# Another order of the opening in a fused retention and two-layer kernel on one core

## The chip, the core and the metric

The kernel runs on one NeuronCore of a Trainium2 chip. The metric is the time of one execution on the device, in microseconds (us). A kernel is run several times, and the median counts; one more execution is recorded by the hardware profiler, and all views of the trace come from that one. Five engines work side by side, each on its own queue and strictly in the order of that queue: TensorE (PE: matrix products), VectorE (DVE), ScalarE (ACT), GpSimd (POOL) and SyncE (SP), which here only issues DMA transfers.

## What is computed

Retention over 4 x 8 heads of 768 tokens and 64 dimensions, and behind it two dense layers with a leaky rectifier between them:

```python
gamma = 1.0 - 2.0 ** (-5.0 - np.arange(H))
scale = 1.0 / np.sqrt(D)
for t in range(S):
    state = gamma[None, :, None, None] * state + np.einsum('bhd,bhe->bhde', k[:, :, t], v[:, :, t])
    y[:, :, t] = scale * np.einsum('bhd,bhde->bhe', q[:, :, t], state)
x = y.transpose(0, 2, 1, 3).reshape(B * S, H * D)      # 3072 x 512
h = x @ w_in                                           # 512 x 2048
g = np.maximum(h, 0.0) + alpha * np.minimum(h, 0.0)
out = g @ w_out                                        # 2048 x 512
```

All inputs and the output are float32 in HBM; products are taken in float16 and summed in float32.

## The kernel before

**Units.** The retention is cut into 24 units `w` (0 to 23). A unit holds 256 tokens of one sequence and four of its eight heads; a pair of units makes 256 tokens, and four units make a block of 512 tokens. There are six blocks. A sequence of 768 tokens is three pairs of units, and a state is handed from pair to pair (and between the two chunks of 128 tokens in a unit).

**What is done for a unit.** `load` fetches k, q and v (256 KB each) through SyncE's queue. `prep` scales k and q into a float16 tile `kdq` (line 189). For units 0 to 7, `turn` brings it into the other layout by eight transposes on TensorE into a PSUM bank `trb` (line 232) and a copy by ScalarE (`kq`, line 238); for later units a DMA transposes. `cast_v` or the last line of `prep` casts v to `vx`. `scores` are 16 small products (line 260) into the PSUM pair `sc`; `masked` multiplies them with a mask on VectorE (line 295). `state_sums` are small products of k and v (line 284), from which `state` makes the carried state on VectorE (lines 309, 311). `within` multiplies masked scores by v into the PSUM pair `y` (line 344) and adds the carried states of one half (line 322); a tiny instruction of another engine, the teller, says that these are through (lines 357, 359); `finish` adds the other half and lets ScalarE copy the result as `xT`, the input of the dense layers (line 373). `visit(w_old, w_new)` runs `within` of an old unit, `scores` and `state_sums` of a new one, `finish` of the old one, then `masked` and `state` of the new one.

**The dense layers of a block.** `ffn1` makes 16 slices `ft` of 128 hidden features; a slice is four products of 128 x 512 (line 427), a rectified copy by ScalarE (line 407) and a combination by VectorE (line 396) into `gt`. `ffn2` makes the four tiles of 128 tokens of the output; a tile is 16 products of 128 x 512 (line 444), one for each slice of `w_out`, summed in one PSUM bank, which ScalarE empties (line 453). Both are generators: `tick(gen, m)` issues the next m products, and so the order of TensorE's instructions is written out by hand, with the units' work between the ticks. In blocks 1 to 5 the next block's units stand between the products of `ffn2`, with fixed numbers of ticks.

**Weights.** `fetch` brings w_in and w_out in 16 pieces of 256 KB each through the same queue of SyncE and in the same staging buffers as k, q and v (eight buffers for each of the three); `cast_w` casts a piece to float16 on GpSimd (line 179). The order of loads in SyncE's queue, and of casts in GpSimd's queue, is that of the program.

**PSUM.** There are eight banks: two single banks named fa and fb, two in a pool "p", and two pairs "s" and "y". The letters in the string given to `ffn1` say which bank each of the 16 slices takes (a capital is the second half of the pair).

**The opening**, lines 467 to 584, is written out unit by unit: units 0 to 3 with turns on TensorE, fills (`busy`, products of ones that nobody reads, line 217) between them, `ffn1(0)` with its first steps between units 2 and 3, then `ffn2(0)` with units 4 to 7 between its products. In `ffn2(0)` tiles 0 and 1 go side by side (one product of each in turn for a slice), then tile 2, then tile 3. The loads stand in the order: w_in, k and q of unit 4, w_out's first four pieces, v of unit 4, the other twelve pieces of w_out, units 5 to 11.

Of the kernel before, what the change touches and what calls it, by code (L numbers as in the profile page):

```python
# [9 lines left out]
FP = mybir.dt.float32  # L10
F16 = mybir.dt.float16
# [7 lines left out]
def kernel(  # L19
# [15 lines left out]
    nc = tc.nc  # L35
# [7 lines left out]
    WB = 4  # L43
# [34 lines left out]
    sbp = ctx.enter_context(tc.tile_pool(name="sbp", bufs=1, space=bass.MemoryType.SB))  # L78
# [6 lines left out]
    ident = mi[:, 256:384]  # L85
    alpha_sb = sbp.tile([NFT, 128], FP, tag="alpha", name="alpha")
    warm = sbp.tile([128, 128], FP, tag="warm", name="warm")[:, 0:1]
    ones = sbp.tile([128, 256], F16, tag="ones", name="ones")[:, 0:128]
    word = sbp.tile([128, 128], FP, tag="word", name="word")[:, 0:1]
    bell = sbp.tile([128, 128], FP, tag="bell", name="bell")[:, 0:1]  # L90
    oma_sb = sbp.tile([128, 128], FP, tag="oma", name="oma")[:, 0:NFT]
# [2 lines left out]

    NPE = 8

    flip = [0]

    def ps(name, tag, n=512, dt=FP, bufs=2):
        if tag == "f":  # L100
            tag = ("fa", "fb")[flip[0] % 2]
            flip[0] += 1
        if tag in ("fa", "fb"):
            bufs = 1
        return psp.tile([128, n], dt, tag=tag, bufs=bufs, name=name)

# [70 lines left out]
    def cast_w(which, i, j):  # L177
        dst, t = pieces[which, i, j]
        nc.gpsimd.tensor_copy(out=dst, in_=t)  # L179
# [33 lines left out]

    def busy(m, at):

        for _ in range(m):
            nc.tensor.matmul(out=at[:, 0:128], lhsT=ones, rhs=ones, start=True, stop=True)

    def cast_v(w):
        vx, v_in = v_ins.pop(w)  # L220
        nc.scalar.activation(out=vx, in_=v_in, func=COPY, bias=0.0, scale=1.0)

    def turn(w, tag, kinds=(0, 1), fill=0):

        kdq, kq, vx = prepped[w]
        flat = kdq.rearrange("p k z r d -> p (k z r d)")
        bank = ps("trb", tag)
        busy(fill, bank)
        trb = bank.bitcast(F16)
        lo, hi = 4 * kinds[0], 4 * kinds[-1] + 4  # L230
        for i in range(lo, hi):
            nc.tensor.transpose(  # L232
                out=trb[:, 128 * i : 128 * i + 128],
                in_=flat[:, 128 * i : 128 * i + 128],
                identity=ident,
            )
        cols = slice(128 * lo, 128 * hi)
        nc.scalar.activation(  # L238
            out=kq.rearrange("p b i -> p (b i)")[:, cols],
            in_=trb[:, cols],  # L240
            func=COPY,
            bias=0.0,
            scale=1.0,
        )
# [25 lines left out]
    sums = {}  # L270
# [2 lines left out]
    def chunks(w):  # L273
        return (0,) if place(w)[3] == NUS - 1 else (0, 1)

    def state_sums(w, cs=None):
        kdq, vx = raw[w]
        for c in cs or chunks(w):
            sums[w, c] = ps(f"st{c}", "p")
        for x in range(2):  # L280
            for a in range(2):
                for c, r in DIAG:
                    if c in (cs or chunks(w)):
                        nc.tensor.matmul(  # L284
                            out=sums[w, c][half(r), 64 * x : 64 * x + 64],
                            lhsT=kdq[half(c), 0, 2 * x + a, r, :],
                            rhs=vx[half(c), 2 * r + x, a, :],
                            start=(a == 0),
                            stop=(a == 1),
                        )  # L290

    def masked(w):
        kdq, kq, vx, sc = live[w]
        m2 = sbp.tile([128, 4, 2, 128], F16, tag="m2", bufs=2, name="m2")
        nc.vector.tensor_tensor(  # L295
            out=m2.rearrange("p s a i -> p s (a i)"),
            in0=sc.rearrange("p (s n) -> p s n", n=256),
            in1=mask.unsqueeze(1).to_broadcast([128, 4, 256]),
            op=MULT,
        )  # L300
        live[w][3] = m2

    def state(w, cs=None):
        u, g, b, c3 = place(w)
        decay = tab[:, 32 + 2 * g : 34 + 2 * g].unsqueeze(2).to_broadcast([128, 2, D])
        for c in cs or chunks(w):
            stv = sums.pop((w, c))[:, 0:128].rearrange("p (x e) -> p x e", e=D)
            if c3 + c > 0:
                nc.vector.tensor_tensor(out=stv, in0=tgs[2 * u + c, g], in1=stv, op=ADD)  # L309
            tg = sbp.tile([128, 4, D], F16, tag="tg", bufs=8, name="tg")[:, 0:2, :]  # L310
            nc.vector.tensor_tensor(out=tg, in0=stv, in1=decay, op=MULT)  # L311
            tgs[2 * u + c + 1, g] = tg
# [20 lines left out]
                    after = None  # L333
        return ins

    def within(w, mid=None, teller=None):
        u, g, b, c3 = place(w)
        vx, m2 = live[w][2:4]
        y = ps("y", "y", 1024, FP, 1)
        started = set()  # L340
        for r in range(2):
            for a in range(2):
                for c, x in DIAG:
                    nc.tensor.matmul(  # L344
                        out=y[half(x), 256 + 256 * c + 128 * r : 384 + 256 * c + 128 * r],
                        lhsT=vx[half(c), 2 * r + x, a, :],
                        rhs=m2[half(c), 2 * r + x, a, :],
                        start=(c, x) not in started,
                        stop=(a == 1 and c3 + c == 0),
                        skip_group_check=True,  # L350
                    )
                    started.add((c, x))
        if mid:
            mid()
        last = carried(w, y, started, True)
        if teller != nc.scalar:
            done = (teller or nc.vector).memset((warm if teller is None else bell)[0:1], 0.0)  # L357
        else:
            done = teller.activation(
                out=word[0:1], in_=word[0:1], func=COPY, bias=0.0, scale=1.0  # L360
            )
        behind(done, last, "tells that the products within the chunks are through")
        live[w].append((y, started, done))

    def finish(w):
        u, g, b, c3 = place(w)
        y, started, done = live[w].pop()
        carried(w, y, started, False, done)
        live.pop(w)
        n, i = divmod(u, 2)  # L370
        if w % WB == 0:
            xT[n] = sbp.tile([128, 2, 4, 2, 128], F16, tag="xT", bufs=2, name=f"xT{n}")
        nc.scalar.activation(  # L373
            out=xT[n][:, g, 2 * i : 2 * i + 2].rearrange("p c r (i a) -> p (c r) i a", a=2),
            in_=y[:, 256:768].rearrange("p (s a i) -> p s i a", a=2, i=64),
            func=COPY,
            bias=0.0,
            scale=1.0,
        )

    def visit(w_old, w_new, cs=None):
        if w_old is not None:
            within(w_old)
        if w_new is not None:
            scores(w_new)
            state_sums(w_new, cs)
        if w_old is not None:
            finish(w_old)
        if w_new is not None:
            masked(w_new)  # L390
            state(w_new, cs)

    gts = {}
# [66 lines left out]
    def tick(gen, m):  # L460
        for _ in range(m):
            if next(gen, 1) == 1:
                return
# [37 lines left out]
    cast_v(1)  # L501
    within(0, teller=nc.scalar)
    turn(2, "f", (0,), fill=4)
    finish(0)
    turn(2, "f", (1,), fill=3)
    state_sums(1)
    prep(3, opening=True, k_on=nc.gpsimd)
    state(1)
    scores(2, fill=8)
    masked(2)  # L510
    within(1, teller=nc.gpsimd)
    for j in range(4):
        cast_w("wi", 0, j)
    cast_v(2)
    turn(3, "f", (0,))
    turn(3, "f", (1,), fill=2)
    finish(1)
    cast_v(3)
# [1 line left out]
    state(2, (0,))  # L520
    scores(3, fill=5)
    masked(3)
    gen = ffn1(0, "ffspypSffYppsfyS", (2, 4))
    within(2, teller=nc.scalar)
    tick(gen, 4)
    finish(2)
    state_sums(3, (0,))
    state(3, (0,))
    tick(gen, 4)
    within(3, mid=lambda: tick(gen, 2))  # L530
    tick(gen, 2)
    finish(3)
    for j in range(4):
        fetch("wi", 3, j)
    load(4, "kq")
    for i in range(4):
        for j in range(4):
            fetch("wo", i, j)
        if i == 0:
            load(4, "v")  # L540
    for w in range(WB + 1, 3 * WB):
        load(w)
    for i in range(1, 4):
        for j in range(4):
# [1 line left out]
    prep(4, opening=True, k_on=nc.gpsimd)  # L546
    for i in range(4):
        for j in range(4):
            cast_w("wo", i, j)

    for _ in gen:
        pass
    turn(4, "p")
    cast_v(4)
    gen = ffn2(0, ((0, 1), (2,), (3,)), ("fa", "fb", "fa", "fb"))
    state_sums(2, (1,))
    state(2, (1,))
    tick(gen, 5)
    state_sums(3, (1,))
    state(3, (1,))  # L560
    visit(None, 4)
    prep(5, opening=True, q_on=nc.vector)
    tick(gen, 27)
    turn(5, "p")
    cast_v(5)
    prep(6, opening=True)
    tick(gen, 5)
    visit(4, 5)
    tick(gen, 3)
    turn(6, "p")  # L570
    cast_v(6)
    prep(7, opening=True)
    tick(gen, 6)
    turn(7, "fb")
    cast_v(7)
    visit(5, 6)
    tick(gen, 9)
    visit(6, 7)
    tick(gen, 5)
    within(7)  # L580
    tick(gen, 2)
    finish(7)
    for _ in gen:
        pass
# [10 lines left out]
    for n in range(1, NBLK):  # L595
        gen = ffn1(n)
# [5 lines left out]
        gen = ffn2(n)  # L602
# [48 lines left out]
```

## Time and profile before

| | before |
|---|---|
| median of 3 runs | 214.1 us (213.47 to 215.0) |
| profiled execution: time | 213.6 us |
| profiled execution: span of its instructions | 211.8 us |
| TensorE busy | 205.5 us (97%) |
| VectorE, ScalarE, GpSimd busy | 125.4, 99.2, 70.9 us |
| HBM read, written | 27.45 MB, 6.29 MB |

The span runs from the first to the last instruction of the program; 1.8 us of the execution's time lie around it. Starts in the views are counted from the beginning of the span. In a row of the order of time stand the start, the length, the engine, the line, the operation, what it writes and reads, shapes, and the count of merged instructions; in brackets the idle time before it and what ended it. TensorE's products are pipelined, so their lengths overlap, and a product of 128 x 512 shows some 0.38 us though the next one starts 0.216 us behind it. So gaps are read from starts, and a busy share of 97% does not say that 97% of the span is needed.

### The profile page before, as it was taken

The page shows a single profiled execution, that of the slowest core. Times are in us where ns is not written, and L with a number is a line of the kernel's source. Part 1 is how long each engine was busy: PE and PEld are TensorE (multiplying, and loading weights), DVE is VectorE, ACT ScalarE, POOL GpSimd, SP SyncE. Part 2 cuts the span into 40 slices and gives each one's busy share as a digit, 9 for nine tenths or more (in the row PEclk, how much of TensorE's full clock was granted, in tenths as well). Part 3 has the DMA queues.
Part 4 walks back from the last instruction along what each step waited for, and adds up shares of the span by engine and source line. Part 5 has one row for each costly group of instructions (what it writes and reads, how often), then busy time and mean ns, then how long its engine had stood idle before and what let it go on. Part 6 is the DMA issues. An engine that isn't in the chain of part 4 may idle for free.

```text
span 211.8 us, 5285 instructions
## 1 busy us (share of the span) xinstructions
PE 205.5 (97%) x2175; PEld 103.8 (49%) x2175; DVE 125.4 (59%) x224; ACT 99.2 (47%) x168; POOL 70.9 (33%) x94
## 2 busy tenths in 40 slices
PE   7999999899999999999999999999999999999992
PEld 8775454364444554444554444554444554444440
DVE  2773986356588733588644588534588733588000
ACT  2685762464765223665223665223665223665121
POOL 0569798349927563544040265000000000000000
PEclk9999999999999999999999999999999999999998
DMA  6999999999999995991364993324500111100111
GB/s 193 348 375 386 304 396 396 300 296 315 321 221 315 274 227 157 263 294 35 88 212 104 218 270 107 89 63 104 147 6 0 50 53 53 50 0 0 53 77 71
DMA packets 63832, 38.28 MB, mean 181 GB/s; under 512 B 19120, under 2 KB 57152, under 8 KB 63808
## 3 DMA queue, kind: packets, MB, share of 16 engines
q1 hardware_dynamic: 63488, 37.76, 62.5%
q8 instruction: 17, 0.28, 0.6%
q10 hardware_dynamic: 320, 0.19, 0.3%
q14 instruction: 7, 0.06, 0.1%
HBM read 27.45 MB, written 6.29 MB: 159 GB/s over the span
## 4 chain that ended last, share of the span: by engine, by line
PE 76%; DMA 13%; POOL 4%; SPq 4%; issue 1%; ACT 0%
PE ops L444 36%; PE hps L427 33%; DMA wo<-in_moe_w_out_dram 6%; SPq L149 4%; PE y L344 3%; DMA wi<-in_moe_w_in_dram 3%; DMA vs<-in_v_dram 3%; PE sc L260 2%; DMA qs<-in_q_dram 2%; POOL win L179 2%; POOL wout L179 1%; PE y L322 1%; PE st L284 1%; POOL kdq L189 1%; ACT os L453 0%
## 5 line engine op out<-in xcount | busy, mean ns | idle before, releaser
L444 PE MATMUL ops<-wout,gt 128*128 128x512 f16 x384 | 89.6, 380 | 0.0
L396 DVE SCALAR_TENSOR_TENSOR gt<-hm,oma,hps 128x512 f16<-128x512 f32 x96 | 71.2, 747 | 28.2 <-ACT hm L407 18.6
L427 PE MATMUL hps<-xT,win 128*128 128x512 f16 (+1 forms) x392 | 84.7, 375 | 0.0
L407 ACT ACTIVATE hm<-hps 128x512 f32<-128x512 f32 x96 | 57.0, 597 | 24.8 <-PE hps L427 24.4
L427 PEld LDWEIGHTS <-win 128*128 128x128 f16 x392 | 37.9, 98 | 44.7 <-issue 0.3
L444 PEld LDWEIGHTS <-gt 128*128 128x128 f16 x384 | 34.9, 98 | 39.8 <-issue 0.5
L189 POOL TENSOR_TENSOR kdq<-ks,tab 128x512 f16<-128x512 f32 x19 | 19.8, 1043 | 42.2 <-DMA ks<-in_k_dram 38.1
L373 ACT ACTIVATE xT<-y 128x512 f16<-128x512 f32 x24 | 14.3, 597 | 40.4 <-PE y L322 40.0
L295 DVE TENSOR_TENSOR m<-sc,mi 128x1024 f16<-128x1024 f32 x24 | 29.3, 1222 | 3.2 <-PE sc L260 1.0
L453 ACT ACTIVATE os<-ops 128x512 f32<-128x512 f32 x24 | 14.2, 597 | 36.1 <-PE ops L444 36.1
L189 POOL TENSOR_TENSOR kdq<-qs,tab 128x512 f16<-128x512 f32 x22 | 23.3, 1058 | 12.0 <-DMA qs<-in_q_dram 12.0
L357 DVE MEMSET warm<- 1x1 f32 x21 | 1.2, 59 | 25.7 <-PE y L322 25.7
L311 DVE TENSOR_TENSOR tg<-st,tab 128x128 f16<-128x128 f32 x40 | 11.6, 289 | 2.0 <-PE st L284 0.9
L322 PE MATMUL y<-kq,tg 64*64 64x128 f16 x160 | 11.5, 228 | 0.0
L179 POOL CAST win<-wi 128x512 f16<-128x512 f32 x16 | 9.8, 613 | 3.3 <-DMA wi<-in_moe_w_in_dram 2.9
L309 DVE TENSOR_TENSOR st<-tg,st 128x128 f32<-128x128 f16 x32 | 9.3, 291 | 2.5 <-PE st L284 0.6
L344 PEld LDWEIGHTS <-vx 64*64 64x64 f16 x384 | 6.4, 106 | 8.6 <-issue 6.6
L260 PE MATMUL sc<-kq 64*64 64x128 f16 x384 | 10.0, 218 | 0.5 <-ACT kq L238 0.3
L238 ACT ACTIVATE kq<-trb 128x512 f16<-128x512 f16 (+1 forms) x12 | 8.6, 735 | 3.5 <-PE trb L232 3.4
L344 PE MATMUL y<-m,vx 64*64 64x128 f16 x384 | 10.0, 221 | 0.1
L179 POOL CAST wout<-wo 128x512 f16<-128x512 f32 x16 | 9.6, 613 | 1.4 <-DMA wo<-in_moe_w_out_dram 1.1
L209 POOL CAST vx<-vs 128x512 f16<-128x512 f32 x16 | 9.8, 610 | 0.5 <-PE ops L444 0.2
(26 smaller groups left out, 66.1 us busy)
## 6 DMA issues: line engine op xcount, KB each, us to landing
ks<-in_k_dram SPq DMA_DIRECT2D x24, 256.0 KB, 4.2
qs<-in_q_dram SPq DMA_DIRECT2D x24, 256.0 KB, 4.6
vs<-in_v_dram SPq DMA_DIRECT2D x24, 256.0 KB, 4.6
out_dram<-os SPq DMA_DIRECT2D x24, 256.0 KB, 2.5
wi<-in_moe_w_in_dram SPq DMA_DIRECT2D x16, 256.0 KB, 5.4
wo<-in_moe_w_out_dram SPq DMA_DIRECT2D x16, 256.0 KB, 5.7
kq<-kdq SPq DMA_TRANSPOSE x16, 4.2
mi<-mi_const ACTq DMA_DIRECT2D x1, 128.0 KB, 2.9
```

The costliest lines, as they stand in the source:

```text
L179: nc.gpsimd.tensor_copy(out=dst, in_=t)
L189: eng.tensor_tensor(out=kdq[:, kind].rearrange("p z r d -> p r z d"), in0=src.rearrange("p (r x) (a d) -> p r (x a) d", a=2, x=2), in1=tab ...
L260: nc.tensor.matmul(out=sc[half(c), at : at + 128], lhsT=kq[half(r), 2 * x + a, half(c)], rhs=kq[half(r), 4 + 2 * x : 6 + 2 * x, half(c)], ...
L295: nc.vector.tensor_tensor(out=m2.rearrange("p s a i -> p s (a i)"), in0=sc.rearrange("p (s n) -> p s n", n=256), in1=mask.unsqueeze(1).to_ ...
L322: ins = nc.tensor.matmul(out=y[half(x), 256 + 256 * c + 128 * r : 384 + 256 * c + 128 * r], lhsT=tgs[2 * u + c, g][half(r), x, :], rhs=kq[ ...
L344: nc.tensor.matmul(out=y[half(x), 256 + 256 * c + 128 * r : 384 + 256 * c + 128 * r], lhsT=vx[half(c), 2 * r + x, a, :], rhs=m2[half(c), 2 ...
L373: nc.scalar.activation(out=xT[n][:, g, 2 * i : 2 * i + 2].rearrange("p c r (i a) -> p (c r) i a", a=2), in_=y[:, 256:768].rearrange("p (s ...
L396: nc.vector.scalar_tensor_tensor(out=gt[:, ft, lo:hi], in0=hm, scalar=oma_sb[:, ft : ft + 1], in1=hps, op0=MULT, op1=ADD,)
L407: nc.scalar.activation(out=hm, in_=hps, func=RELU, bias=0.0, scale=-1.0)
L427: nc.tensor.matmul(out=hpss[ft][:, 128 * lo : 128 * hi], lhsT=w_in_all[:, hp, 128 * ft : 128 * ft + 128], rhs=xT[n][:, hp // 2, lo:hi, hp ...
L444: nc.tensor.matmul(out=opss[tq], lhsT=gt[:, ft, 128 * tq : 128 * tq + 128], rhs=w_out_all[:, ft, :], start=(ft == 0), stop=(ft == NFT - 1),)
L453: nc.scalar.activation(out=os_sb, in_=opss[tq], func=COPY, bias=0.0, scale=1.0)
```

## The change

It has these parts:

- **Fills:** four fills of 128 columns become one of 512 (`ones` is 512 wide), and some counts change.
- **PSUM names:** "p" becomes two single banks pa and pb in turn, which may also be named one by one; `state_sums` takes a bank or a slice of one, and `within` may use the pair "s".
- **Opening of units 0 to 3:** unit 2's second turn goes ahead of `finish(0)`, unit 3's first turn ahead of `scores(2)`; unit 2's v is cast by GpSimd; `within(3)` uses the pair "s", and the banks of `ffn1(0)` are strung in another order.
- **Loads and casts:** unit 5's k, q and v go ahead of w_out's last four pieces, unit 6's k and q between the two halves of these, and v of units 6 and 7 behind k and q of unit 7. The last two pieces of w_out are cast behind unit 6's preparation; the v of units 6 and 7 are cast by GpSimd.
- **`ffn2(0)`:** tiles 0, 1 and 2 side by side, then tile 3 in tile 0's bank; the second chunks' states of units 2 and 3 go together behind nine products; other numbers of ticks; `visit(4, 5)` makes the state ahead of the mask (`early`).

```diff
-    flip = [0]
+    flip = {"f": False, "p": False}
     def ps(name, tag, n=512, dt=FP, bufs=2):
-        if tag == "f":
-            tag = ("fa", "fb")[flip[0] % 2]
-            flip[0] += 1
-        if tag in ("fa", "fb"):
+        if tag in ("s", "y"):
+            n, bufs = 1024, 1
+        if tag in flip:
+            flip[tag] = not flip[tag]
+            tag += "ba"[flip[tag]]
+        if tag in ("fa", "fb", "pa", "pb"):
             bufs = 1
...
-        for _ in range(m):
-            nc.tensor.matmul(out=at[:, 0:128], lhsT=ones, rhs=ones, start=True, stop=True)
+        for n in [512] * (m // 4) + [128] * (m % 4):
+            nc.tensor.matmul(
+                out=at[:, 0:n], lhsT=ones[:, 0:128], rhs=ones[:, 0:n], start=True, stop=True
+            )
...
     turn(2, "f", (0,), fill=4)
+    turn(2, "f", (1,), fill=2)
     finish(0)
-    turn(2, "f", (1,), fill=3)
     state_sums(1)
     prep(3, opening=True, k_on=nc.gpsimd)
     state(1)
-    scores(2, fill=8)
+    turn(3, "f", (0,), fill=4)
+    scores(2, fill=2)
     masked(2)
     within(1, teller=nc.gpsimd)
+    cast_v(2, on_pool=True)
     for j in range(4):
         cast_w("wi", 0, j)
-    cast_v(2)
-    turn(3, "f", (0,))
     turn(3, "f", (1,), fill=2)
...
-    gen = ffn1(0, "ffspypSffYppsfyS", (2, 4))
+    gen = ffn1(0, "ffyppsYffSppyfsY", (2, 4))
...
-    within(3, mid=lambda: tick(gen, 2))
+    within(3, mid=lambda: tick(gen, 2), pair="s")
...
     for i in range(4):
+        if i == 3:
+            load(5, "kqv")
         for j in range(4):
+            if (i, j) == (3, 2):
+                load(6, "kq")
             fetch("wo", i, j)
         if i == 0:
             load(4, "v")
-    for w in range(WB + 1, 3 * WB):
+    load(7, "kq")
+    load(6, "v")
+    load(7, "v")
+    for w in range(2 * WB, 3 * WB):
         load(w)
...
-            cast_w("wo", i, j)
+            if i < 3 or j < 2:
+                cast_w("wo", i, j)
...
-    turn(4, "p")
+    turn(4, "pb")
     cast_v(4)
-    gen = ffn2(0, ((0, 1), (2,), (3,)), ("fa", "fb", "fa", "fb"))
-    state_sums(2, (1,))
-    state(2, (1,))
-    tick(gen, 5)
-    state_sums(3, (1,))
-    state(3, (1,))
-    visit(None, 4)
+    gen = ffn2(0, ((0, 1, 2), (3,)), ("pa", "fa", "fb", "pa"))
+    tick(gen, 9)
+    st = ps("st", "y")
+    state_sums(2, (1,), st[:, 0:512])
+    state_sums(3, (1,), st[:, 512:1024])
+    scores(4)
+    state_sums(4, None, "pb")
+    for w in (2, 3, 4):
+        state(w, (1,) if w < 4 else None)
+    masked(4)
     prep(5, opening=True, q_on=nc.vector)
-    tick(gen, 27)
-    turn(5, "p")
+    tick(gen, 24)
+    turn(5, "y")
     cast_v(5)
     prep(6, opening=True)
+    for j in (2, 3):
+        cast_w("wo", 3, j)
+    tick(gen, 6)
+    visit(4, 5, None, "pb", True)
+    tick(gen, 3)
+    turn(6, "pb")
+    prep(7, opening=True)
+    cast_v(6, on_pool=True)
+    cast_v(7, on_pool=True)
+    tick(gen, 8)
+    visit(5, 6, None, ("pb", "fa"))
+    tick(gen, 3)
+    turn(7, "fb")
     tick(gen, 5)
-    visit(4, 5)
-    tick(gen, 3)
-    turn(6, "p")
-    cast_v(6)
-    prep(7, opening=True)
-    tick(gen, 6)
-    turn(7, "fb")
-    cast_v(7)
-    visit(5, 6)
-    tick(gen, 9)
-    visit(6, 7)
-    tick(gen, 5)
+    visit(6, 7, None, ("pb", "fa"))
+    tick(gen, 4)
     within(7)
-    tick(gen, 2)
+    tick(gen, 1)
     finish(7)
```

## What I predicted

> **What bounds the kernel now.** I read the busy time of stretches first. In each row the first number is the length, then come the engines' busy times with their instructions.
>
> ```profile
> 31.02:52.99 21.97, 21.04 (x313) 11.03 (x312) 12.74 (x28) 10.23 (x16) 15.04 (x21) 1.00 1.05 329
> 53.16:208.13 154.97, 154.96 (x1472) 73.12 (x1470) 92.53 (x160) 68.94 (x117) 36.01 (x42) 1.00 0.51 132
> ```
>
> From 53.16 us, where block 1's first product starts, TensorE is busy 154.96 of 154.97 us at granted clock 1.00. The change leaves the order of TensorE's instructions there as it was (the ring of single-bank tiles turns as the old pool did), so I cost that part at nothing: its cover is TensorE itself. Only the time at which block 1 starts can move. Next, the chain that ended last (start, length, what) and SyncE's queue:
>
> ```profile
> 29.46 5.89 DMA wo<-in_moe_w_out_dram
> ...
> 40.14 4.56 DMA qs<-in_q_dram
> ...
> 53.16 13.81 PE hps L427 x64
> ```
>
> ```profile
> 25.42 7.71 SPq L174 DMA_DIRECT2D wo<-in_moe_w_out_dram  x12
> ```
>
> 64 products take 13.81 us, so 0.216 us each when dense. The chain in front of 53.16 runs over loads: w_out, then unit 7's q, landing at 44.70. Loads land in the order in which SyncE issues them, about one per 0.64 us for w_out (7.71 / 12). The stage that the change rewrites is block 0's second product. TensorE's order of time, columns start, length, instruction, idle before and its releaser:
>
> ```profile
> 31.02 0.61 PE L232 MATMUL trb<-mi,kdq 128*128 128x128 f16 x8
> ...
> 33.54 6.25 PE L444 MATMUL ops<-wout,gt 128*128 128x512 f16 x27
> 39.97 0.40 PE L232 MATMUL trb<-mi,kdq 128*128 128x128 f16 x4 [0.18 <-DVE kdq L189]
> ...
> 40.96 1.24 PE L444 MATMUL ops<-wout,gt 128*128 128x512 f16 x5
> 42.13 0.42 PE L344 MATMUL y<-m,vx 64*64 64x128 f16 x16
> ...
> 43.05 0.82 PE L444 MATMUL ops<-wout,gt 128*128 128x512 f16 x3
> 43.71 0.61 PE L232 MATMUL trb<-mi,kdq 128*128 128x128 f16 x8
> 44.16 1.46 PE L444 MATMUL ops<-wout,gt 128*128 128x512 f16 x6
> 45.45 0.39 PE L232 MATMUL trb<-mi,kdq 128*128 128x128 f16 x4
> ...
> 46.51 0.42 PE L344 MATMUL y<-m,vx 64*64 64x128 f16 x16
> ...
> 47.36 2.12 PE L444 MATMUL ops<-wout,gt 128*128 128x512 f16 x9
> 49.41 0.42 PE L344 MATMUL y<-m,vx 64*64 64x128 f16 x16
> ...
> 50.24 1.25 PE L444 MATMUL ops<-wout,gt 128*128 128x512 f16 x5
> 51.43 0.42 PE L344 MATMUL y<-m,vx 64*64 64x128 f16 x16
> ...
> 52.99 1.24 PE L427 MATMUL hps<-xT,win 128*128 128x512 f16 x5
> ```
>
> Lengths overlap, so I go by starts. A turn of a unit costs 44.16 - 43.71 = 0.45 us when nothing is late. 27 products from 33.54 should end at 39.37, but the products after turn(5) begin at 40.96: 1.59 - 0.45 = 1.14 us of stall (w_out's last casts and unit 5's k and q). Five products take 42.13 - 40.96 = 1.17, 0.09 over 5 x 0.216, which is the price of a step from products to the 64-row kind. Turn(7) takes 46.51 - 45.45 = 1.06; less 0.45 and that 0.09, 0.52 is stall (unit 7's q). So 1.66 us of the 21.97 is waiting for loads and their casts.
>
> **Stalls removed: -1.66.** VectorE and GpSimd show when those loads were there:
>
> ```profile
> 39.22 0.69 DVE L189 TENSOR_TENSOR kdq<-ks,tab 128x512 f16<-128x512 f32 x1 [3.53 <-DMA ks<-in_k_dram]
> ```
>
> ```profile
> 35.40 3.74 POOL L179 CAST wout<-wo 128x512 f16<-128x512 f32 x6 [0.69 <-DMA wo<-in_moe_w_out_dram]
> 42.32 1.04 POOL L189 TENSOR_TENSOR kdq<-qs,tab 128x512 f16<-128x512 f32 x1 [3.19 <-DMA qs<-in_q_dram]
> 44.76 1.37 POOL L189 TENSOR_TENSOR kdq<-qs,tab 128x512 f16<-128x512 f32 x1 [1.40 <-DMA qs<-in_q_dram]
> ```
>
> Unit 5's k is there at 39.22 and unit 6's q, four loads behind, at 42.32: 0.77 us per unit load. In the new order k, q and v of unit 5 go ahead of w_out's last group. One more piece of w_out follows the one that landed at 29.46 + 5.89 = 35.35; counting on by 0.64 and 0.77 gives k5 36.8, q5 37.5, v5 38.3, the next two of w_out 38.9 and 39.6, k6 40.3, q6 41.0. By the last two of w_out the same nine loads have passed as before by q6, so the last lands at 42.3. Likewise v6 stands where q7 stood, at 44.70, with q7 near 44.0 and v7 0.8 to 1.3 later. The buffers that these loads take over were emptied by w_in's, unit 4's and w_out's first casts, all before 35.40, so SyncE's queue gets no new wait ahead of them.
>
> Who needs them: with three tiles side by side slice ft of w_out is needed at step 3 ft, not 2 ft. GpSimd's queue is now: w_out 3_1 (cast by 40.2, one cast 3.74 / 6 = 0.62), unit 6's q (41.0 to 42.1), w_out 3_2 and 3_3 (by 43.3), unit 7's q, casts of v6 and v7. Behind unit 6's q wait two casts of w_out, which TensorE needs only at about 43.1 and 43.7.
>
> **The opening: -0.26.** ScalarE is where its last link lies:
>
> ```profile
> 14.97 0.63 ACT L221 ACTIVATE vx<-vs 128x512 f16<-128x512 f32 x1
> 15.68 0.20 ACT L359 ACTIVATE word<-word 1x1 f32<-1x1 f32 x1
> 16.34 0.60 ACT L373 ACTIVATE xT<-y 128x512 f16<-128x512 f32 x1 [0.46 <-PE y L322]
> ```
>
> ```profile
> 9.56 0.47 SPq L149 DMA_DIRECT2D vs<-in_v_dram  x1
> ```
>
> ```profile
> DMA to landing us min/median/max: 5.4/5.4/5.4
> ```
>
> ```profile
> 16.04 0.25 PE L322 MATMUL y<-kq,tg 64*64 64x128 f16 x4
> ...
> 16.99 0.42 PE L344 MATMUL y<-m,vx 64*64 64x128 f16 x16
> ...
> 18.35 11.97 PE L427 MATMUL hps<-xT,win 128*128 128x512 f16 x56
> ```
>
> Moving turns 2 and 3 forward and unit 2's cast to GpSimd brings scores(3) and within(2) some 0.4 to 0.6 us forward, but v3 lands at 9.56 + 5.4 = 14.96; its cast and then the teller (0.20) are still queued on ScalarE, so finish(2) comes at about 15.88 instead of 16.04: 0.16. within(3) waited for xT(2) to leave the y pair (16.34 + 0.60 = 16.94, start 16.99); put into the other pair it starts when TensorE reaches it: 0.10 more. Ends: 0, if v3's cast slips, and 0.6, if it doesn't bind. I take 0.26, nearest to the cast's row. Fills hold TensorE's waits and cost nothing while they end before their data. Block 0's first product is dense behind that, so the stage starts at 30.76. The new order of its PSUM banks reuses none closer than three slices, as before.
>
> **Two steps fewer: -0.18.** 9, then 24 products in place of 5 and 27, with the state sums gathered, save two 0.09 changes of kind. Running on from 30.76: first products and sums 3.20, 24 products 5.18, turn(5) at 39.14, six products, visit at 40.97 (0.92 as at 42.13 to 43.05), three products, turn(6) at about 42.6.
>
> **Waits added: +1.1.** First, tile 3 takes the bank of tile 0. Rows of ScalarE:
>
> ```profile
> 44.36 1.02 ACT L238 ACTIVATE kq<-trb 128x1024 f16<-128x1024 f16 x1 [0.59 <-PE trb L232]
> ...
> 48.54 0.60 ACT L453 ACTIVATE os<-ops 128x512 f32<-128x512 f32 x1
> ...
> 52.66 0.60 ACT L373 ACTIVATE xT<-y 128x512 f16<-128x512 f32 x1 [1.69 <-PE y L322]
> ```
>
> ScalarE starts unit 6's copy 44.36 - 43.71 = 0.65 behind the turn, so 43.3 to 44.3; then it empties tile 0 in 0.60. Tile 0's last product starts at 43.7, tile 3's first would at 44.35 (three products), and gets the bank at about 44.8: +0.48, with turn(7) and all visits queued behind it on TensorE. Ends: 0 (an emptied bank in time) and 1.1 (one more copy ahead). Turn(6) waits some 0.1 for unit 5's state to leave its bank.
>
> Second, the tail:
>
> ```profile
> 50.15 1.22 DVE L295 TENSOR_TENSOR m<-sc,mi 128x1024 f16<-128x1024 f32 x1
> ...
> 52.24 0.06 DVE L357 MEMSET warm<- 1x1 f32 x1
> ```
>
> Before, behind the start of visit(6,7) at 49.41 lay 9 products; now 6, so that start lies 3 x 0.216 = 0.65 nearer the end in work. But its chain is as long: mask 50.15 to 51.37, the teller at 52.24, xT(7) until 52.66 + 0.60 = 53.26, which unit 7's half of block 1 needs. Before, that half started at 52.99 + 2 x 0.216 = 53.42, 4.01 behind the visit; the chain needs 3.91. The shorter work can win 0.10 of its 0.65, the rest is waiting: +0.55 (ends 0.3 and 0.65).
>
> The cast of v6 on GpSimd (0.62) starts behind unit 7's q. I take that row at 1.37, not 1.04, since VectorE prepares unit 7's k at the same time here too: 44.0 to 45.3, cast until 45.95, and visit(5,6), begun at 45.4, asks for it at about 45.95. At 1.04 it has 0.3 to spare. The Trainium skill (SBUF — State Buffer, Who interferes with whom) says that a VectorE instruction with two SBUF inputs and a GpSimd one that reads SBUF shut each other out. By that rule whole instructions add, 1.04 + 0.69 at the worst, and the sum would lose another 0.36 us; the row's 1.37 shows half of that.
>
> Sum: -1.66 - 0.26 - 0.18 + 0.48 + 0.10 + 0.55 = -0.97. The profiled execution took 213.6 (span 211.8, 1.8 around it); it becomes 212.6. The median shown, 214.1, lies 0.5 above that execution, so I forecast 213.1.
>
> **Rivals.**
> *More is won* (chance 0.10): tile 0's bank is empty in time and the opening gives its 0.6. -0.97 - 0.48 - 0.34 = -1.8: 212.3. Against: 1.05 us from tile 0's last product to its empty bank, and only 0.65 of cover.
> *Nothing is won* (0.13): w_out's last two casts, now behind unit 6's q in GpSimd's queue, or unit 5 land a load or two later than counted, and 0.6 to 1.2 of the stalls come back at another place: about 214.1.
> *Slower* (0.11): v6 is the late load. TensorE stands in visit(5,6) for it, and tile 3 and units 6 and 7 behind it. It decides from a landing at 44.7: each us later costs one. With the 5.89 of the w_out row in place of 4.56, it lands 1.33 later: +0.36, 214.5; a load behind that, 215.2. For it: the queue has no slack. Against: the same bytes are ahead of it as of q7 before.
> *Cold start* (0.06): `ones` is four times as wide.
>
> ```profile
> 0.84 0.17 DVE L467 MEMSET ones<- 128x128 f16 x1 [0.84 <-PEq L635]
> ...
> 1.06 3.81 PE L217 MATMUL trb<-ones 128*128 128x128 f16 x34 [1.06 <-DVE word L479]
> ```
>
> The first fills take 3.81 us for 34, 0.11 each for 128 columns, where dense products take 0.216 for 512: they run at half speed. At four times 0.17, TensorE starts 0.5 later; if full speed comes later too, the early turns slip, and what GpSimd's preparation of unit 3 doesn't hide I put at 0 to 1.2 us, say 0.6: 213.7. The Trainium skill (TensorE: Matmul & The Clock Gate, Part 1: The HAM clock gate) has full speed follow from about 3.4 us of activity in a window that runs freely. By that rule a late start can miss a whole window; the row agrees as far as it goes, with half speed through all of its 3.81 us.
>
> **How the numbers follow.** My forecast has 0.60. Its own range, by the ends of the bank, tail and opening terms, is -1.8 to +0.0: 212.3 to 214.1. Leaving out the far ends of the rivals, 8 in 10 lie in 212.0 to 214.7. One per cent, 2.1 us, is about what a measurement of this kernel tells from no change (its runs span 213.5 to 215.0). A gain of 2.1 needs every added wait to be nearly free: 0.06. A loss of 2.1 needs v6 late by three us or a late load with a cold start: 0.08. Within: 0.86.
>
> **What would show it.** Right: no idle in front of turn(5) and turn(7); a gap of about 0.5 in front of tile 3's first product, ended by ScalarE; short gaps in front of within(7) and finish(7); block 1's start near 52.0. Wrong: TensorE idle in visit(5,6) for a cast of GpSimd; w_out casts that end a wait of the second product; unit 5's k later than 37.5; anything that moves behind block 1's start.

## The result, and the profile after

| | before | after |
|---|---|---|
| median of 20 runs each | 214.9 us (213.43 to 216.19) | 213.72 us (212.59 to 216.03) |
| ratio, 95% interval | | 0.9955 [0.9933, 0.9977] |
| profiled execution: time, span | 213.6, 211.8 us | 213.77, 212.0 us |

The changed kernel is 0.45% faster by the ratio, 0.97 us of 214.9, with an interval of 0.5 to 1.4 us; the two medians lie 1.18 us apart. The two profiled executions, laid side by side, say the opposite: 0.17 us slower. Both are right. The profiled execution of before lies 1.3 us under the median of its kernel, that of after on the median of its own. So the comparison has to go stage by stage, and has to ask of each stage whether it differs with the kernel or from run to run. (The ratios are taken over undisturbed runs, and the first profile of v3_early, for which TensorE was granted 0.984 of its full clock, is not compared with the others.)

The stretches of after, in the same columns as before the change:

```profile
32.09:53.02 20.93, 20.32 (x313) 10.90 (x312) 12.85 (x28) 8.99 (x14) 15.65 (x22) 1.00 1.08 344
53.24:208.20 154.96, 154.96 (x1472) 73.09 (x1470) 92.55 (x160) 69.06 (x117) 36.30 (x42) 1.00 0.51 133
```

Block 0's second product, from unit 4's first transposition to block 1's first product, takes 20.93 us for 21.97. From block 1 on nothing moved: 154.96 for 154.97. But the second product begins at 32.09, not 31.02; the opening took 1.07 us more in this execution. TensorE's order of time after the change:

```profile
35.22 5.35 PE L455 MATMUL ops<-wout,gt 128*128 128x512 f16 x24
40.41 0.61 PE L239 MATMUL trb<-mi,kdq 128*128 128x128 f16 x8
40.86 1.46 PE L455 MATMUL ops<-wout,gt 128*128 128x512 f16 x6
...
44.24 1.46 PE L455 MATMUL ops<-wout,gt 128*128 128x512 f16 x6
46.01 0.59 PE L455 MATMUL ops<-wout,gt 128*128 128x512 f16 x2 [0.30 <-ACT os L464]
...
48.03 0.61 PE L239 MATMUL trb<-mi,kdq 128*128 128x128 f16 x8
48.48 1.24 PE L455 MATMUL ops<-wout,gt 128*128 128x512 f16 x5
...
51.68 0.42 PE L352 MATMUL y<-m,vx 64*64 64x128 f16 x16 [0.16 <-DVE m L303]
...
52.62 0.24 PE L330 MATMUL y<-kq,tg 64*64 64x128 f16 x2 [0.15 <-DVE warm L365]
...
53.02 0.59 PE L438 MATMUL hps<-xT,win 128*128 128x512 f16 x2
```

24 products from 35.22 end at 35.22 + 24 x 0.216 = 40.40, and turn(5) follows at 40.41; turn(7) takes 0.45 and has nothing in front of it. Both stalls of before are gone. What is new is the row at 46.01: six products from 44.24 should end at 45.54, so 0.47 us pass before tile 3's first product, and ScalarE's emptying of a bank ends the wait. Two smaller gaps follow at the end, ended by VectorE's mask and by its teller. ScalarE beside it:

```profile
44.44 1.02 ACT L245 ACTIVATE kq<-trb 128x1024 f16<-128x1024 f16 x1 [0.63 <-PE trb L239]
45.36 1.57 ACT L464 ACTIVATE os<-ops 128x512 f32<-128x512 f32 x3
```

Three tiles are emptied in one go, right behind unit 6's copy; tile 3 needs the first of the three banks.

### The profile page after: what moved, and what is told of

It reads as the page before. It is cut to its first block, busy times and chain, and to the rows that moved or that the text cites. A ratio compares the mean times of both kernels' runs of the same rounds, so it can differ in the third digit from the quotient of the medians.

```text
span 212.0 us, 5174 instructions
## 1 busy us (share of the span) xinstructions
PE 204.0 (96%) x2121; PEld 99.1 (47%) x2121; DVE 125.7 (59%) x224; ACT 97.6 (46%) x165; POOL 72.2 (34%) x97
## 4 chain that ended last, share of the span: by engine, by line
PE 88%; SPq 4%; DMA 3%; ACT 1%; DVE 1%; issue 1%; DVEq 0%
PE ops L455 39%; PE hps L438 39%; SPq L151 4%; PE y L352 3%; DMA vs<-in_v_dram 3%; PE sc L267 2%; PE y L330 2%; PE st L292 1%; PE trb L239 1%; DVE m L303 1%; SPq L176 1%; ACT os L464 1%; ACT kq L245 0%; DVE tg L319 0%; DVE st L317 0%
```

## The experiments

Twelve runs were made. Where a time is given with an interval, it is the ratio to the kernel before, run on the same chip. Three figures are read from each profile: when unit 3's v landed (SyncE's issue plus its time to landing), how far behind that block 0's dense products start, and the length of the second product's stretch.

| kernel | opening | second product | v3 landed | dense start behind it | stretch | ratio |
|---|---|---|---|---|---|---|
| before | old | old | 14.94 | 3.40 | 21.97 | 1 |
| after | new | new | 16.42 | 3.00 | 20.93 | 0.9955 [0.9933, 0.9977] |
| changed_again | new | new | 15.53 | 3.00 | 20.92 | |
| late_half | old | new | 15.60 | 3.50 | 20.93 | 0.9926 [0.9892, 0.9959] |
| opening_half | new | old | 15.29 | 3.00 | 22.12 | 0.9981 [0.9947, 1.0014] |
| narrow_fills | new, old fills | new | 15.68 | 3.00 | 20.92 | 0.9932 [0.9896, 0.9967] |
| tiles_alone | new | new, old loads | 16.88 | 3.00 | 22.87 | |
| loads_alone | new | old, new loads | 17.44 | 3.00 | 26.55 | |
| bank_out | new | bank's wait out | 16.70 | 3.00 | 21.67 | |
| both_waits_out | new | both waits out | 15.37 | 3.00 | 20.18 | 0.9874 [0.9836, 0.9912] |
| both_waits_again | new | both waits out | 15.63 | 3.00 | 20.09 | 0.9877 [0.9835, 0.9919] |
| old_opening | old | both waits out | 15.67 | 3.39 | 20.10 | 0.9916 [0.9879, 0.9954] |

The dense products themselves took 12.67 us in every one of them, and from block 1's third product to the last of all 154.29 to 154.31 us passed.

### Which half: late_half and opening_half

late_half is the changed kernel with everything from `prep(0)` to `finish(3)` as before, and the old fills; opening_half is the opposite cut, with loads, casts and second product as before.

> Only the second half of the change: loads, casts and block 0's second product as after the change, the opening of units 0 to 3, its fills and the banks of block 0's first product as before. Theory 1 (the gain lies in block 0's second product, the opening varies with the landing of its loads): the stretch from the first transposition of unit 4 to the first product of block 1, 21.97 us before and 20.93 after the change, is 20.8 to 21.1 here, and the time is 0.7 to 1.2 us under the kernel before. Theory 2 (the new opening costs the 1.07 us by which block 0's dense products start later in the profile after, 19.42 for 18.35, and the second half wins twice that): the time is about 2 us under the kernel before.

> Only the first half of the change: fills, order of units 0 to 3 and banks of block 0's first product as after the change, loads, casts and block 0's second product as before. Theory 1: the stretch of the second product stays at about 22.0 us, the time lies within 0.5 us of the kernel before. Theory 2: 1 us slower than before. If the opening brings what the prediction said: 0.26 us faster, which these rounds can hardly tell from nothing.

```profile
31.77:52.70 20.93, 20.32 (x313) 10.89 (x312) 12.67 (x28) 8.99 (x14) 15.83 (x22) 1.00 1.08 347
```

```profile
30.96:53.08 22.12, 21.19 (x314) 11.03 (x312) 12.76 (x28) 10.25 (x16) 16.53 (x22) 1.00 1.09 346
```

The first row is late_half's stretch, the second opening_half's: 20.93 and 22.12. The stretch goes with the second half of the change and with nothing else. In time late_half wins 0.74%, 1.6 us, more than the 0.7 to 1.2 expected; its interval, 0.9 to 2.3 us, holds the 0.45% of the whole change and also the 2 us of theory 2, so this time alone decides nothing. opening_half does: it isn't told apart from no change, and its interval ends at 0.3 us slower, so the 1 us of theory 2 is out. The 1.07 us of the profile pair is no price of the new opening.

### The late start: narrow_fills

```diff
-        for n in [512] * (m // 4) + [128] * (m % 4):
-            nc.tensor.matmul(out=at[:, 0:n], lhsT=ones[:, 0:128], rhs=ones[:, 0:n], ...)
+        for _ in range(m):
+            nc.tensor.matmul(out=at[:, 0:128], lhsT=ones, rhs=ones, start=True, stop=True)
```

> The changed kernel with the old fills: 128 columns each, and a tile of ones of 128 columns. TensorE starts at about 1.06 us as before the change, not at 1.46. If the late start matters (theory 2, and the cold start of the prediction), the time falls by 0.4 us or more against the changed kernel, to 1.4 us or more under the kernel before. If the loads set the opening (theory 1), it stays at 0.7 to 1.2 us under the kernel before.

The rows that belong to it, of the changed kernel: VectorE's fill of `ones`, then TensorE's first work.

```profile
0.91 0.48 DVE L478 MEMSET ones<- 128x512 f16 x1 [0.91 <-PEq L660]
```

```profile
1.46 3.53 PE L219 MATMUL trb<-ones 128*128 128x512 f16 x10 [1.46 <-DVE word L490]
4.83 0.39 PE L239 MATMUL trb<-mi,kdq 128*128 128x128 f16 x4
5.05 0.38 PE L219 MATMUL trb<-ones 128*128 128x512 f16 x1
5.73 0.28 PE L239 MATMUL trb<-mi,kdq 128*128 128x128 f16 x2 [0.30 <-DVE kdq L191]
```

TensorE starts 0.40 later than before, and at 5.73 it waits for unit 0's q all the same. The time does not decide: with the old fills the ratio is 0.9932, 1.46 us under the kernel before and so just past the mark set for "the late start matters", with the new ones it is 0.9955, and the intervals overlap. The profiles do: with either fills the dense products start 3.00 us behind v3's landing. By the clock records of the traces the granted clock was full from 5.63 us on in before, from 4.58 in after, and in the nine profiles of the new opening from anywhere between 3.98 and 7.50, always with the same 3.00. The late start costs nothing that can be seen.

### What sets the opening: old_opening, v3_early, changed_again

old_opening is both_waits_out (below) with the old opening and fills.

> The kernel of the run both_waits_out with the old opening of units 0 to 3 (fills, order, banks of block 0's first product). In four profiles of the new opening block 0's dense products start 3.00 us behind the landing of unit 3's v, in two of the old one 3.41 and 3.50. If that is the opening's gain, this profile shows 3.4 to 3.5, the stretch of the second product 20.2, and the time is 0.3 to 0.6 us above that of both_waits_out, so about 2.1 us under the kernel before. If the opening gains nothing, it is the same as both_waits_out.

The profile came as expected: 3.39 behind v3, beside 3.40 and 3.50 in the other two with the old opening and 3.00 in nine with the new one. The new opening is 0.43 us shorter (the mean 3.43 less 3.00) when measured from v3. In time it is not seen: 0.9916 against 0.9874 and 0.9877 points the same way, late_half's 0.9926 against the 0.9955 of the whole change points the other way, and in each case the intervals overlap. ScalarE in old_opening shows where the 0.43 lies:

```profile
13.67 0.63 ACT L226 ACTIVATE vx<-vs 128x512 f16<-128x512 f32 x1 [0.88 <-DMA vs<-in_v_dram]
14.20 1.07 ACT L243 ACTIVATE kq<-trb 128x512 f16<-128x512 f16 x2
15.16 0.60 ACT L379 ACTIVATE xT<-y 128x512 f16<-128x512 f32 x1
15.70 0.63 ACT L226 ACTIVATE vx<-vs 128x512 f16<-128x512 f32 x1
16.39 0.20 ACT L365 ACTIVATE word<-word 1x1 f32<-1x1 f32 x1
```

In the old opening ScalarE waits for unit 2's v, and unit 3's two copies and xT(1) queue behind its cast; unit 3's v is cast without a wait for it, as soon as ScalarE is free. So it is unit 2's v that the old opening hangs on: its dense products start 5.42, 5.62 and 5.42 us behind that landing in before, late_half and old_opening. In all three, unit 3's v came 2.0 to 2.1 us behind unit 2's, and the 0.43 holds for that distance; no run has the old opening with unit 3's v as late as the 3.6 us of the first profile of after. In the changed kernel the cast of unit 2's v has gone to GpSimd, and ScalarE waits for unit 3's v:

```profile
16.44 0.63 ACT L228 ACTIVATE vx<-vs 128x512 f16<-128x512 f32 x1 [1.19 <-DMA vs<-in_v_dram]
16.98 0.19 ACT L367 ACTIVATE word<-word 1x1 f32<-1x1 f32 x1
```

```profile
17.21 0.25 PE L330 MATMUL y<-kq,tg 64*64 64x128 f16 x4 [0.35 <-ACT word L367]
...
19.42 0.39 PE L438 MATMUL hps<-xT,win 128*128 128x512 f16 x1
```

From v3's landing to the first dense product it is always 3.00 us. Would an earlier v3 bring the start forward? v3_early is both_waits_out with this:

```diff
-    for w, which in (..., (3, "kq"), (2, "v")):
+    for w, which in (..., (3, "kq"), (2, "v"), (3, "v")):
...
-            if (i, j) == (0, 2):
-                load(3, "v")
```

> The kernel of the run both_waits_out with unit 3's v loaded two places earlier, ahead of the first two pieces of w_in, which come one place later each. If v3's landing alone sets when block 0's dense products start (3.00 us behind it in eight profiles), the start moves with it: two places of 0.65 to 0.75 us, about 1.4 us earlier, and the time is 3 to 4 us under the kernel before. If the stream of loads as a whole sets it, the first products now wait for the casts of w_in's first pieces, the start stays within 0.4 us of where it was, some 4.3 us behind v3's landing, and the time is like that of both_waits_out.

> The kernel of the run v3_early, whose profiled execution was a disturbed one with a lower granted clock, profiled once more. If the stream of loads sets the start, block 0's dense products start 3.0 us or a little less behind the landing of w_in's second piece, which now takes the place that unit 3's v had in the queue, and more than 4 us behind unit 3's v; if v alone did, 3.00 us behind that.

The time, 0.9928 [0.9886, 0.9969], isn't better than that of both_waits_out, let alone by the 1.4 us that an earlier start would have brought. In the second profile v3 landed at 13.94, and the dense products started at 19.66, 5.72 behind it where some 4.3 were expected. TensorE there:

```profile
16.49 0.39 PE L438 MATMUL hps<-xT,win 128*128 128x256 f16 x2 [0.43 <-POOL win L181]
17.13 0.39 PE L438 MATMUL hps<-xT,win 128*128 128x256 f16 x2 [0.25 <-POOL win L181]
```

Now the casts of w_in's first two pieces end the waits; the second landed at 16.41, and the start is 3.25 behind that, a little more than the 3.0 expected. So in this one profile v3 no longer sets the start, and the next loads of the stream do: v3 was only the last of it that something waited for.

> The changed kernel as it is, profiled once more: the stretch of the second product 20.9 to 21.0 us whatever the loads of the opening do, block 0's dense products 3.00 us behind unit 3's v, and 154.3 us from block 1's third product to the last one.

changed_again met all three: 20.92, 3.00, and 154.29 us. Its v3 landed at 15.53, 0.89 earlier than in the first profile of the same kernel. The landing alone moves the profiled time by that much; in the profile of before it came at 14.94, the earliest of the twelve in the table. The profile pair comes out of this: 1.47 us later by the landing, 0.40 less behind it, and 0.94 less up to block 1's third product leave the changed kernel's span 0.13 us longer, of the 0.17 by which the times differ.

### Which part of the second half: tiles_alone and loads_alone

tiles_alone takes the changed kernel and puts loads and casts back into the old order; loads_alone keeps their new order and puts tiles, ticks and banks of `ffn2(0)` back.

> The changed kernel with the old order of loads and casts: w_out whole ahead of units 5 to 7, all its casts ahead of unit 5's preparation. If the new order of loads is what takes the stalls at turn(5) and turn(7) away, they come back: unit 5's q is prepared about 9.6 us behind the first transposition of unit 4 (40.7 for 31.0 before the change), TensorE asks for it at 8.3, so 1.0 to 1.3 us idle at turn(5), and the stretch of the second product is 21.8 to 22.3 us for 20.93. If three tiles side by side take them away by themselves, the stretch stays under 21.2.

> The changed kernel with the old second product (tiles 0 and 1 side by side, old ticks and banks) and the new order of loads and casts. Two tiles need the last slices of w_out two thirds of the way earlier: slice 14 is asked for about 7.8 us behind the first transposition of unit 4 and cast at about 11.6. If the three tiles are what makes the later w_out bearable, TensorE stands 3 to 4 us before slices 14 and 15, and the stretch of the second product is 23.5 to 25 us. If the loads alone do it, the stretch is about 21.

tiles_alone, VectorE and TensorE:

```profile
41.54 0.69 DVE L191 TENSOR_TENSOR kdq<-ks,tab 128x512 f16<-128x512 f32 x1 [3.10 <-DMA ks<-in_k_dram]
```

```profile
42.29 0.40 PE L239 MATMUL trb<-mi,kdq 128*128 128x128 f16 x4 [1.26 <-DVE kdq L191]
43.02 0.40 PE L239 MATMUL trb<-mi,kdq 128*128 128x128 f16 x4 [0.34 <-DVE kdq L191]
```

loads_alone, TensorE:

```profile
41.79 1.23 PE L455 MATMUL ops<-wout,gt 128*128 128x512 f16 x4 [1.89 <-POOL wout L181]
...
44.60 1.64 PE L455 MATMUL ops<-wout,gt 128*128 128x512 f16 x4 [1.58 <-POOL wout L181]
```

Neither wins anything alone: 22.87 and 26.55 us for 21.97, each in a single execution and each above its expected range. With the old loads unit 5 is late at turn(5), 1.92 us by starts for the 1.0 to 1.3 expected. Unit 5's k landed 8.97 us behind the start of the stretch here, and 8.18 and 8.33 in before and opening_half, so 0.6 to 0.8 us of that is this execution's late loads; without them I estimate a stretch of 22.1 to 22.2, like that of neither part. With the old tiles the last slices of w_out are late, 2.05 and 1.74 us by starts; up to 1.7 us of the 26.55 come from a lower granted clock, of which more at the end. The three tiles are what pays for the earlier units; the loads are what makes use of it.

### The two waits that the change adds: both_waits_out, both_waits_again, bank_out

```diff
-    gen = ffn2(0, ((0, 1, 2), (3,)), ("pa", "fa", "fb", "pa"))
+    gen = ffn2(0, ((0, 1, 2), (3,)), ("pa", "fa", "fb", "fa"))
...
-    tick(gen, 8)
-    visit(5, 6, None, ("pb", "fa"))
-    tick(gen, 3)
+    tick(gen, 6)
+    visit(5, 6, None, ("pb", "pa"))
+    tick(gen, 2)
...
-    visit(6, 7, None, ("pb", "fa"))
-    tick(gen, 4)
+    visit(6, 7, None, ("pb", "pa"))
+    tick(gen, 5)
     within(7)
-    tick(gen, 1)
+    tick(gen, 2)
```

To this comes unit 6's v ahead of unit 7's k and q, in the loads and in GpSimd's queue. bank_out is the first part alone: the other bank, 6 and 5 products around visit(5, 6), ticks of the tail and loads as in the changed kernel.

> The changed kernel without the two waits that its profile shows in block 0's second product: tile 3 takes the bank of tile 1 and starts two products later, behind visit(5, 6), whose second sums take tile 0's bank; two products less stand ahead of visit(6, 7) and three more behind it; v of unit 6 is loaded and cast ahead of k and q of unit 7. If the bank (0.47 us idle before tile 3's first product) and the tail (0.55 us) are what they seem, the stretch of the second product falls from 20.93 to 19.9 to 20.2 us and the time to 1.7 to 2.2 us under the kernel before. If the loads are the real bound there, TensorE waits instead in visit(5, 6) for the cast of unit 6's v or in front of turn(7), and the stretch stays at 20.6 or more.

> The kernel of the run both_waits_out once more on another chip: 1.7 to 2.7 us under the kernel before if its gain holds, the stretch of the second product 20.1 to 20.3 us, and block 0's dense products 3.00 us behind the landing of unit 3's v.

> The changed kernel with the bank's wait alone taken away: tile 3 in tile 1's bank and two products later, behind visit(5, 6); products ahead of visit(6, 7) and behind it as after the change. The idle 0.47 us before tile 3's first product goes; if the loads allow, the stretch falls from 20.93 to 20.4 to 20.6 us. The tail's three gaps (0.23, 0.22, 0.10) stay. If unit 6's v is the next limit, 0.1 to 0.4 us of idle time appears in visit(5, 6) before the sums of unit 6.

```profile
31.04:51.22 20.18, 20.18 (x313) 10.79 (x312) 12.95 (x28) 9.10 (x14) 14.92 (x21) 1.00 1.07 343
```

In both_waits_out TensorE has work in progress for 20.18 of 20.18 us. The bank's wait and the tail's are gone, and the kernel beats the one before and the changed one: 0.9874 and 0.9877 on two chips, 2.6 to 2.7 us with intervals of 1.7 to 3.6. The stretch gives 1.8 to 1.9 of it, the opening some 0.4 where unit 3's v comes as in before; the rest I can't place, and the intervals allow for it. bank_out missed its 20.4 to 20.6 us:

```profile
47.65 0.32 PE L292 MATMUL st<-vx,kdq 64*64 64x64 f16 x16 [0.73 <-POOL vx L226]
```

The bank's wait is gone there too, but TensorE then stands for GpSimd's cast of unit 6's v, 0.90 us by starts, more than the 0.47 won (a further 0.32 behind turn(6), for a cast of w_out, is new as well). The changed kernel's bank wait had covered that load. This is a single execution with late loads (v3 at 16.70), and they explain the 0.32: that cast of w_out ended 12.41 us behind the start of the stretch here, and 11.56 to 11.86 in the four profiles that have the changed second product with its loads. They explain little of the 0.90: set the ends of unit 6's cast in those four against TensorE asking 0.47 and two products earlier, and I estimate a wait of 0.7 to 0.8 in each. So taking the bank's wait out alone should not pay; with unit 6's v loaded and cast earlier it does.

## Why the prediction was right

The forecast of 0.97 us less is what was measured, 0.45% of 214.9. That it fits to the hundredth is luck: the interval is 0.5 to 1.4 us, and by the stages more was won than forecast, 0.94 us for 0.71 in the second product and some 0.4 for 0.26 in the opening. What holds is the mechanism. Its steps:

- **Stalls removed, -1.66:** both gone, as the rows at 40.41 and 48.03 show. That it takes tiles and loads together, as the argument with slice ft at step 3 ft said, is shown by tiles_alone and loads_alone. One sign of being wrong did come in the first profile of after, unit 5's k at 38.02 for 37.5, with the late stream of loads; turn(5) wanted it only at 40.41. In changed_again it landed at 36.70, and block 1 started at 52.12, near the 52.0 forecast, for 53.02 in after.
- **Tile 0's bank, +0.48:** 0.47, ended by ScalarE as described.
- **Tail, +0.55:** idle by starts are 0.23 before within(7), 0.22 before finish(7) and 0.10 before block 1's third product: 0.55. The chain behind visit(6,7) was put at 3.91 us, where the rows shown for it, 49.41 to 53.26, give 3.85 without the step to TensorE; measured from 49.65 to block 1's third product at 53.56 it is 3.91.
- **Changes of kind, -0.18, and turn(6), +0.10:** here the stretch was mis-sized. Up to block 1's third product it was to become 0.71 us shorter (the sum of 0.97 less the opening's 0.26) and became 0.94 shorter. The wait of turn(6) for unit 5's state did not come (0.46 for the turn), the first products and sums took 35.22 - 32.09 = 3.13 for 3.20, and the visit of unit 5 took 43.09 - 42.25 = 0.84 for 0.92.
- **The opening, -0.26:** the bound by v3's landing was right, the size was 0.40 to 0.43 where v3 comes 2.0 us behind unit 2's v. The other pair for within(3) gave its 0.10 (0.85 us from finish(2)'s products to within(3) for 0.95), but finish(2) won 0.31 for 0.16: it starts 0.79 us behind v3's landing, 1.10 in before. The step took v3 for the bound of the old opening also; there it was unit 2's v, cast on ScalarE ahead of three other copies. In time this part remains within the noise.
- **The base:** 213.1 was forecast and 213.72 measured, because 214.1, the median of three runs, was 0.8 below that of twenty.

Of the rivals, *more is won* needed tile 0's bank to be free, and it was not. *Slower*, with unit 6's v late, did not happen in the three profiles that have the changed second product with its loads (after, late_half, narrow_fills) nor in changed_again, but it is what bank_out ran into. *Nothing is won* did not happen either: no cast of w_out ends a wait in the second product of these four, though one does in bank_out. *Cold start* falls by the 3.00 us and the clock records beside narrow_fills. For the port that VectorE and GpSimd share, the row of unit 7's q in the changed kernel is between the two figures weighed:

```profile
45.17 1.19 POOL L191 TENSOR_TENSOR kdq<-qs,tab 128x512 f16<-128x512 f32 x1 [0.66 <-DMA qs<-in_q_dram]
```

1.19 us is 0.15 over 1.04. VectorE's preparation of unit 7's k had begun 0.40 us earlier, so the two ran together for 0.29 us only; in before it was 0.46, with 0.32 over. In late_half, narrow_fills and opening_half it was 0.49, 0.52 and 0.65, and GpSimd took 1.39, 1.42 and 1.55: each time 1.04 plus the shared time less 0.14. In changed_again GpSimd began first, by 0.03 us:

```profile
43.85 1.04 POOL L191 TENSOR_TENSOR kdq<-qs,tab 128x512 f16<-128x512 f32 x1 [0.53 <-DMA qs<-in_q_dram]
43.88 1.56 DVE L191 TENSOR_TENSOR kdq<-ks,tab 128x512 f16<-128x512 f32 x1
```

There GpSimd kept its 1.04, and VectorE took 1.56 for 0.69. So of these two instructions the one that begins second waits for the other, as the Trainium skill's rule (SBUF — State Buffer, Who interferes with whom) has it, and the row of 1.37 showed half of the worst case because the two overlapped by no more than that.

## What to carry to other kernels

Compare profiles by stages, and tie each stage to the event that releases it (here the landing of one load): a stage that varies with its loads by a microsecond hides a change of the same size in the whole time. Where loads come in one stream, ask in which order their data is needed and change the order of use with the order of loads; one alone can win nothing, or be worse than neither. When a stall is removed, count what covered it: the products that were taken from the tail, and the bank that was handed on at once, gave back 1.0 of 1.66 us, and putting three products and one bank elsewhere, with one load moved ahead, won most of it back.

## What the runs showed of the hardware

In loads_alone, TensorE's granted clock fell to half, though it was never idle for long:

```profile
46.80:48.80 2.00, 2.00 (x8) 0.68 (x6) 0.00 (x0) 1.68 (x3) 0.86 (x2) 0.50 0.96 285
```

The clock record has 0.50 for 3.41 us from 45.48 on, and the products there start 0.43 us apart. In the five microseconds ahead of it lie the idle times of 1.89 and 1.58 us shown above. The Trainium skill (TensorE: Matmul & The Clock Gate, Why this matters for your kernels) warns of idle gaps over about 3 us; neither of these was as long. That they made the clock fall was not tried, and these traces give no threshold: in tiles_alone idle times of 1.26 and 0.34 us left the clock at 1.00, while in the first profile of v3_early it fell to 0.50 at 17.61, for 6.83 us, with 0.34 and 1.08 us of idle time just ahead.

Loads mostly land 0.62 to 0.76 us apart, but now and then one is 1.1 to 2.0 us behind the one before it. In the profiles of before and after, one 16 KB packet of the instruction queue starts one to three microseconds ahead of six of the ten that come behind the third load and in the first 50 us (for instance at 10.42 and 22.52 us before landings at 12.93 and 24.64; at 13.24 and 34.83 before 15.75 and 37.36). In the twelve profiles of the table, counted the same way, it is so for 27 of 39, and 19 such packets have no late landing behind them. That these fetches hold up one of the 16 DMA engines, and with it the load, would fit the former, but no run tried it.
